# DeltaNet into a noisy top-2 router on one core: own tiles for the first expert's early rows, two tiles of inverses, and a remade plan

## The chip, the cores and the metric

The kernel runs on one core of a Trainium2 chip. The time is device microseconds from the start of the program to its end on that core, a median over runs. One more execution is recorded by the hardware profiler; its own time stands beside the span that its trace covers. All data are fp32.

## The reference

The first half is a DeltaNet recurrence for 4 batches of 8 heads, 768 tokens and head width 48. Its output, laid out as 3072 tokens of 384 numbers, goes to a router with 8 experts, of which each token takes two.

```python
# attention: one state of D x D for each batch and head
k_n = k / (norm(k) + 1e-6)
for t in range(S):
    y[t] = q[t] @ state                     # read before the update
    state += beta[t] * outer(k_n[t], v[t] - k_n[t] @ state)
# router and experts
x = y, as (3072, 384)
noisy = x @ w_gate + log1p(exp(x @ w_noise)) * noise
top2 = the two largest of the 8; weights = softmax over these two
out[token] += weight * (relu(x[token] @ w1[e]) @ w2[e])     # w1: 384 x 1024, w2: 1024 x 384
```

## The kernel before

**Attention.** A chunk holds 64 tokens, there are 12 chunks, and a unit is one chunk of two batches (all their heads), so there are 24 units; four units make a step, `s`, of which there are six. For each step the kernel forms products of the keys (`products`, L558 transposes and L576 matmuls on TensorE, copies at L565, L609 and L615 on ScalarE), and inverts 32 x 32 triangular blocks on VectorE (`begin_inversion`, `invert`, `end_inversion`): one transpose into the tile `t` (L626), a norm (L644 to L665, of which L654 needs `root` from ScalarE, L648 and L649), 30 columns of two operations each (L704, L708), a scaling (L720), and two transposes out (L730 into `tb`, L738 into `tt`). `join` (L761 to L799) puts two such blocks together; `within` gives the masked products of queries and keys (L824); `recur` runs the recurrence (L845 to L928: `solve` is L890, `gather_state` is L912, the state is added at L924), two units at a time; `answer` gives y and the router's logits (L949 to L991; L964 is the matmul of the logits).

**Routing.** `route(g)` turns the logits of one or two steps into experts, weights and row numbers, on VectorE with short matmuls (L1081 to L1087). `spread` (L383, GpSimd) scatters each unit's rows twice, once for each expert, into `rows_x` in device memory: 48 scatters of 128 rows, 1552 bytes each. `cut(s, rows)` makes sure that expert 0 has `rows` rows by then, so that they may be used early.

**Early rows.** `early(s)` takes the first 128-row tiles of expert 0 as soon as the rows of the steps up to `s` are there: load (L1246), transpose (L1274), `hidden = relu(w1 rows)` (L1300, L1310), back through `w2` (L1323), weighting (L1337) and a scatter into the output (L424). In this kernel it works in tiles of the keys and queries that are no longer needed, four tiles at a time and then one:

```python
EARLY = {3: (0, 4), 4: (4, 5)}
xr = old_k[0:4]
xe = [*old_kT[0:2], old_q[0]]
hT = old_k
```

**Order.** Nothing is issued in the order of the source. Each piece is a job with an engine, an estimated cost, what it reads and writes, and a due time; `Jobs.order` simulates the engines with these estimates and writes the order of each engine's queue once, when the program is built. Its constants are `FIRST`, `PACE`, `BEHIND` (due times of inverses and of routing), `SIGNAL` (time from one engine to another), `PATIENCE` and `SOON`. Jobs with `late` set, as those of the early rows, go behind all others that could start. On the chip each engine takes its queue in that order, and a job that waits holds up all behind it; GpSimd's and SyncE's queues are planned in the same way.

**Experts.** After attention, `rest` does the remaining rows of expert 0 and experts 1 to 7 follow, each as a seven-product scheme of block matrices (L1548).

Of the kernel before, what the change touches and what calls it, by code (L numbers as in the profile page):

```python
# [21 lines left out]
Q = 32  # L22
TILES = 6
MORE = 64
EARLY = {3: (0, 4), 4: (4, 5)}
ROWS = TILES * 128 + MORE
ROW = 384 + 4
# [4 lines left out]
FIRST, PACE, BEHIND = 13.0, 36.0, 100.0  # L32
# [60 lines left out]
class Jobs:  # L93
# [8 lines left out]
    SIGNAL = 0.15  # L102
# [5 lines left out]
    def add(self, engine, cost, emit, reads=(), writes=(), opens=None, uses=None, closes=None,  # L108
            lands=0.0, moves=0.0, due=None, late=None, apart=0.0):
        job = SimpleNamespace(  # L110
            engine=engine, cost=cost, emit=emit, opens=opens, closes=closes, lands=lands,
# [105 lines left out]
    PATIENCE = 0.05  # L217
    SOON = 3.0
# [14 lines left out]
def kernel(  # L233
# [148 lines left out]
    def spread(rows, slot, cleared):  # L382
        d = nc.gpsimd.indirect_dma_start(  # L383
            out=rows_x,
            out_offset=bass.IndirectOffsetOnAxis(ap=slot, axis=0),
            in_=rows,
            in_offset=None,
        ).ins
        tc.declare_no_dep(d, group="spread", reason="no two tokens have the same row")
        tc.add_to_no_dep_group("spread", d)  # L390
        for i in cleared:
            tc.add_manual_dep(d, i.name, SYNC, reason="rows cleared before they are written")
        written.append(d)
        return d
# [35 lines left out]
    def deltanet(ictx):  # L430
# [34 lines left out]
        NK, NT_, NW = 3 * US, 3 * US, US + NU  # L465

        NQ, N_U, N_ST = 3 * NU, 2 * NU, 2
# [19 lines left out]
        two_gds = ring([128, UH, Q], "gd", 2)  # L487
        most_steps = max(x for _, x in INVERSIONS)
        inversion_of = {s + x: g for g, (s, n) in enumerate(INVERSIONS) for x in range(n)}
        t_inv = sb([128, most_steps, Q, Q], "t")  # L490
# [94 lines left out]
        def products(n):  # L585
# [15 lines left out]
            gd = two_gds(s).rearrange("p (u j z) i -> p u z j i", u=US, z=2)[:, i]  # L601
            for x, lo in enumerate(range(0, 128, Q)):
# [9 lines left out]
                    writes=[("gd", s % 2, i, lo)], uses=p,  # L612
# [6 lines left out]
        def begin_inversion(s):  # L619
# [3 lines left out]
            gd = two_gds(s)  # L623
# [5 lines left out]
                reads=[("gd", s % 2, i, lo) for i in range(US) for lo in range(0, 128, Q)],  # L629
                writes=["t"], due=FIRST + first_s * PACE + 2 * x,  # L630
            )

        def invert(g):

            first_s, steps = INVERSIONS[g]
            t, v_ = t_inv[:, 0:steps], nc.vector
            diagonal = t.rearrange("p s i j -> p s (i j)")[:, :, 0 : Q * Q : Q + 1]
            ss, root, norm, d, minus_d = (x[:, 0:steps] for x in small.values())
# [28 lines left out]
            jobs.add(DVE, 0.4, squares, reads=["t"], writes=["ss", "root"], due=soon)  # L667
            jobs.add(ACT, 0.5, by_log, writes=["root"], due=soon + 1)

            for x in range(steps):  # L670
# [6 lines left out]
                    reads=["ss"], writes=["t"], due=soon + 3,  # L677
# [3 lines left out]
                DVE, 2.0, lengths, reads=["root", "ss", *every_beta], writes=["norm", "d"],  # L681
                due=soon + 3,
            )
            for x in range(steps):
                jobs.add(
                    DVE, 0.2,
                    lambda x=x: v_.transpose(out=norms(first_s + x), in_=norm[:, x]),
                    reads=["norm"], writes=[("norms", (first_s + x) % 3)],
                )
# [5 lines left out]
                reads=["d"], writes=["t"],  # L695
# [16 lines left out]
            for j in range(1, Q - 1):  # L712
                jobs.add(
                    DVE, 0.36 + 0.0019 * steps * j * (Q - 1 - j), lambda j=j: column(j),
                    writes=["t", *(("column", first_s + x, j) for x in range(steps))],
                )
            jobs.add(DVE, 0.2, lambda: v_.memset(diagonal, 1.0), writes=["t"])
# [5 lines left out]
                reads=["d"], writes=["t"],  # L723
            )

        def end_inversion(s):
            x = s - INVERSIONS[inversion_of[s]][0]
# [6 lines left out]
                reads=["t"], writes=["tb"],  # L734
# [6 lines left out]
                reads=["t"], writes=["tt"],  # L741
            )

        def join(units):
# [21 lines left out]
            for n, m in zip([*units, None], [None, *units]):  # L766
# [34 lines left out]
                jobs.add(PE, 0.65, products_of, reads=reads, opens=p)  # L801
# [134 lines left out]
        def answer(n, bank_y):  # L936
# [64 lines left out]
            x: sb([128, most_steps, Q], x) for x in ("ss", "root", "norm", "d", "minus_d")  # L1001
# [13 lines left out]
        def route(g):  # L1015
# [151 lines left out]
            for x in range(units):  # L1167
                of, i = first_s + x // US, x % US
                for to in slot:
# [4 lines left out]
                            [y for name in clears for y in cleared[name]],  # L1174
# [35 lines left out]
        def flat(t):  # L1210
            return t.rearrange("p h d -> p (h d)")

        def key_of(name, i, size):
            return halves(name, i % size) if name in ("k", "q") else [(name, i % size)]

        def early(s):
# [4 lines left out]
            lo, hi = EARLY[s]  # L1221
            n, rows = hi - lo, (hi - lo) * 128
            first_unit = (NS - 1) * US
            old_k = [(flat(kps(first_unit + US + i)), halves("k", (first_unit + US + i) % NK))
                     for i in range(NK - US)]
            old_kT = [(flat(kTs(first_unit + US + i)), [("kT", (first_unit + US + i) % NT_)])
                      for i in range(NT_ - US)]
            old_q = [(flat(qps(i)), halves("q", i % NQ)) for i in range(NQ)]
            if lo == 0:
                xr = old_k[0:4]  # L1230
                xe = [*old_kT[0:2], old_q[0]]
                hT = old_k
                xr = [(x[:, 0:ROW], key) for x, key in xr]
                hT = [(x[:, 0:rows], key) for x, key in hT]
            else:
                (x, key), (y, key_y), *z = old_kT[2:6]
                xr = [(x[:, 0:ROW], key)]
                xe = [(y[:, do * 128 : (do + 1) * 128], key_y) for do in range(KT)]
                hT = [
                    (z[fo // 4][0][:, fo % 4 * 128 : (fo % 4 + 1) * 128], z[fo // 4][1])  # L1240
                    for fo in range(FT)
                ]

            def load_rows(i):
                r0 = (lo + i) * 128
                d = nc.sync.dma_start(out=xr[i][0], in_=rows_x[r0 : r0 + 128]).ins  # L1246
                for w in written:
                    tc.add_manual_dep(d, w.name, SYNC, reason="rows of the tokens so far")

# [3 lines left out]
            ]  # L1253
            for i in range(n):
                at = lo + i
                jobs.add(
                    SP, 0.7, lambda i=i: load_rows(i), reads=of_steps,
                    writes=[*xr[i][1], ("xr", at)], lands=2.0, moves=0.7, late=lo,
                )

                def of_rows(i=i, at=at):
                    x = xr[i][0]
# [4 lines left out]
                    DVE, 0.5, of_rows, reads=[("xr", at), *xr[i][1]], writes=[("gate", at)],  # L1267
                    late=lo,
                )
                p = Bank(2, (0, 1))  # L1270

                def turned_rows(i=i, p=p):
                    for do in range(KT):
                        nc.tensor.transpose(  # L1274
                            p.tile[:, 0, do * 128 : (do + 1) * 128],
                            xr[i][0][:, do * 128 : (do + 1) * 128], ident,
# [3 lines left out]
                    PE, 0.5, turned_rows, reads=[("xr", at), *xr[i][1]], opens=p, late=lo,  # L1280
                    writes=[k for x in xe for k in x[1]],
                )

                def copied(i=i, p=p):
                    for do in range(KT):
                        nc.scalar.copy(
                            xe[do][0][:, i * 128 : (i + 1) * 128],
                            p.tile[:, 0, do * 128 : (do + 1) * 128],
                        )

                jobs.add(
                    ACT, 0.9, copied,
                    writes=[("xe", at), *(k for x in xe for k in x[1])], closes=p, late=lo,
                )
            for fo in range(FT):
                p = Bank(2, (0, 1))
                for do in range(KT):
                    jobs.add(
                        PE, 0.0017 * rows,
                        lambda fo=fo, do=do, p=p: nc.tensor.matmul(  # L1300
                            p.tile[:, 0, 0:rows], w1e[:, do, fo * 128 : (fo + 1) * 128],
                            xe[do][0][:, 0:rows], start=(do == 0), stop=(do == KT - 1),
                        ),
                        reads=[("xe", lo + i) for i in range(n)] + xe[do][1], late=lo + 0.1,
                        writes=hT[fo][1] if do == 0 else [],
                        **({"uses": p} if do else {"opens": p}),
                    )
                jobs.add(
                    ACT, 0.08 + rows * 0.0011,
                    lambda fo=fo, p=p: nc.scalar.activation(  # L1310
                        hT[fo][0], p.tile[:, 0, 0:rows], ACTF.Relu
                    ),
                    writes=[("hT", lo, fo), *hT[fo][1]], closes=p, late=lo + 0.1,
                )
            for i in range(n):
                at = lo + i
                p = Bank(2, (0, 1))
                got, got_key = old_q[1 + at % 3]
                for f0 in range(0, FT, 2):

                    def back(i=i, p=p, f0=f0):
                        for fo in (f0, f0 + 1):
                            nc.tensor.matmul(  # L1323
                                p.tile[:, 0, 0:DM], hT[fo][0][:, i * 128 : (i + 1) * 128],
# [4 lines left out]
                        PE, 1.3, back, late=lo + 0.2, writes=[] if f0 else got_key,  # L1329
                        reads=[  # L1330
                            x for fo in (f0, f0 + 1) for x in (("hT", lo, fo), *hT[fo][1])
                        ],
# [5 lines left out]
                        got[:, 0:DM], p.tile[:, 0, 0:DM], early_gate[:, at : at + 1]  # L1338
                    ),
                    reads=[("gate", at)], writes=got_key, closes=p, late=lo + 0.2,  # L1340
# [50 lines left out]
        for s in range(NS):  # L1391
# [33 lines left out]
            if s in EARLY:  # L1425
                cut(s, EARLY[s][1] * 128)
# [475 lines left out]
```

## Time and profile before

| what | us |
|---|---|
| median of 3 runs | 885.67 |
| lowest and highest run | 878.36, 887.37 |
| the profiled execution's own time | 881.57 |
| its span | 879.8 |
| TensorE, VectorE, ScalarE, GpSimd busy | 753.7, 564.0, 332.4, 357.0 |
| last matmul of logits (L964) ends | 361.4 |
| early rows on TensorE | 369.0 to 426.3 |
| rest of expert 0 | 427.1 to 447.2 |
| experts 1 to 7 | 447.2 to the end |

Times inside the execution are counted from the start of its span. Engines are PE (TensorE), PEld (its weight loads), DVE (VectorE), ACT (ScalarE), POOL (GpSimd) and SP (SyncE). In the row of slices each digit stands for a fortieth of the span, 22 us. A wait is put down to the engine whose signal came last; "issue" and "remote" are stretches in which the trace shows nothing that the engine waited for, or nothing that it can name.

### The profile page before, as it was taken

How to read it: one execution, taken by the hardware profiler on the slowest of the kernel's cores; microseconds unless marked ns; L12 is line 12 of the kernel's file. 1: busy time of each engine (PE TensorE's matmuls, PEld its weight loads, DVE VectorE, ACT ScalarE, POOL GpSimd, SP SyncE). 2: the span in 40 equal slices, each digit the busy share in tenths (PEclk: the TensorE clock that was granted, in tenths of full speed). 3: DMA queues.
4: the chain of work that ended last, by engine and by line, in shares of the span. 5: the costliest groups of instructions: out<-in, count | busy, mean ns of one | idle time of the engine just before them, and what ended most of it. 6: DMA issues, size and time to landing. Idle time of an engine off the chain costs nothing.

```text
span 879.8 us, 22711 instructions
## 1 busy us (share of the span) xinstructions
PE 753.7 (86%) x9462; PEld 584.6 (66%) x9462; DVE 564.0 (64%) x1297; ACT 332.4 (38%) x791; POOL 357.0 (41%) x372
## 2 busy tenths in 40 slices
PE   3678578765579768799999999999999999999995
PEld 2467467665368657546757858859769678688594
DVE  5889786878559563301479658577587586585651
ACT  3675665735355234220334153152151341431510
POOL 1020202010540341421257487477577675773611
PEclk8578777655859756599999999999999999999998
DMA  2465986833421211371173242433423331401201
GB/s 48 76 122 124 296 179 139 227 83 85 156 80 36 71 65 39 114 261 59 41 256 105 96 145 72 138 104 120 137 80 132 120 104 37 143 3 53 60 19 40
DMA packets 119855, 93.80 MB, mean 107 GB/s; under 512 B 85414, under 2 KB 110023, under 8 KB 119744
## 3 DMA queue, kind: packets, MB, share of 16 engines
q1 hardware_dynamic: 108016, 64.54, 26.6%
q0 software_dynamic: 9552, 27.33, 9.2%
q8 instruction: 76, 1.25, 0.6%
q10 hardware_dynamic: 2176, 0.39, 0.3%
q14 instruction: 35, 0.29, 0.1%
HBM read 58.82 MB, written 34.81 MB: 106 GB/s over the span
## 4 chain that ended last, share of the span: by engine, by line
PE 61%; DVE 13%; issue 7%; ACT 5%; SPq 5%; another core or an unknown queue 4%; POOL 2%; DMA 2%; POOLq 0%; DVEq 0%; ACTq 0%
PE inner L1548 24%; PE outer L1548 14%; DVE part L704 3%; DVE t L708 3%; PE pair L1300 3%; PE pair L1323 3%; PE inner L1653 2%; PE inner L1580 2%; SPq L526 2%; SPq L377 2%; PE pair L890 1%; PE pair L949 1%; PE single L558 1%; PE pair L576 1%
## 5 line engine op out<-in xcount | busy, mean ns | idle before, releaser
L1607 DVE TENSOR_TENSOR hT<-hT,inner 128x416 f32<-128x416 f32 x182 | 105.5, 586 | 61.5 <-PE inner L1548 52.0
L1613 ACT ACTIVATE hT<-inner 128x416 f32<-128x416 f32 x112 | 57.9, 517 | 171.3 <-PE inner L1548 169.1
L424 POOL DMA_INDIRECT out_dram<-sums,index x49 | 50.8, 1037 | 113.7 <-DVE sums L1448 105.3
L673 POOL TENSOR_SCALAR_AFFINE_SELECT t<-t 128x1024 f32<-128x1024 f32 x6 | 7.6, 1266 | 180.9 <-DVE ss L644 180.9
L1548 PE MATMUL inner<-s_x,w1e 128*128 128x416 f32 x196 | 78.7, 512 | 0.0
L1448 DVE SCALAR_TENSOR_TENSOR sums<-outer,gate,sums 128x192 f32<-128x192 f32 x112 | 45.2, 414 | 50.2 <-PE outer L1548 50.1
L708 DVE TENSOR_TENSOR t<-t,part 128x30 f32<-128x30 f32 (+9 forms) x180 | 61.1, 339 | 6.2
L1602 ACT ACTIVATE hT<-hT 128x416 f32<-128x416 f32 x112 | 59.9, 547 | 12.2 <-DVE hT L1607 6.7
L704 DVE TENSOR_TENSOR part<-t 128x30 f32<-128x30 f32 (+9 forms) x180 | 60.2, 334 | 5.1
L1548 PE MATMUL outer<-t_w,hT 128*128 128x192 f32 x336 | 59.7, 328 | 0.0
L383 POOL DMA_INDIRECT rows_x<-y,slot x48 | 46.8, 975 | 28.8 <-issue 11.3
L415 POOL DMA_INDIRECT sums<-out_dram,index x49 | 52.5, 1072 | 13.9 <-issue 13.0
L1548 PE MATMUL inner<-xe,w1e 128*128 128x416 f32 x140 | 58.1, 513 | 0.0
L1548 PEld LDWEIGHTS inner<-s_x,w1e 128*128 128x128 f32 x196 | 37.2, 190 | 31.2 <-issue 29.8
L1548 PE MATMUL inner<-s_x,s_w 128*128 128x416 f32 x140 | 56.9, 512 | 0.0
L1548 PEld LDWEIGHTS outer<-t_w,hT 128*128 128x128 f32 x336 | 54.7, 190 | 0.4
L1585 ACT COPY xe<-inner 128x384 f32<-128x384 f32 (+1 forms) x49 | 20.1, 462 | 85.4 <-PE inner L1580 85.4
L1548 PE MATMUL outer<-w2e,hT 128*128 128x192 f32 x280 | 50.1, 326 | 0.0
L1548 PEld LDWEIGHTS outer<-w2e,hT 128*128 128x128 f32 x280 | 46.5, 190 | 2.2 <-issue 2.2
L1514 POOL TENSOR_TENSOR w1e<-w1e 128x256 f32<-128x256 f32 x54 | 46.3, 867 | 2.0
L558 PE MATMUL single<-ident,kp 128*128 128x128 f32 x96 | 22.7, 380 | 23.7 <-DMA kp<-in_k_dram 14.7
L1548 PEld LDWEIGHTS inner<-s_x,s_w 128*128 128x128 f32 x140 | 26.6, 190 | 22.3 <-issue 22.3
(220 smaller groups left out, 1650.8 us busy)
## 6 DMA issues: line engine op xcount, KB each, us to landing
w1e<-in_moe_w_dram SPq DMA_DIRECT2D x8, 1536.0 KB
w2e<-in_moe_w_dram SPq DMA_DIRECT2D x8, 1536.0 KB
xr<-rows_x SPq DMA_DIRECT2D x7, 1164.0 KB
rows_x<-empty SPq DMA_DIRECT2D x8, 776.0 KB
v<-in_v_dram SPq DMA_DIRECT2D x48, 96.0 KB
qp<-in_q_dram SPq DMA_DIRECT2D x48, 96.0 KB
out_dram<-empty SPq DMA_DIRECT2D x4, 1152.0 KB
kp<-in_k_dram SPq DMA_DIRECT2D x88, 48.0 KB
```

The lines of the kernel that those rows point to most:

```text
L383: d = nc.gpsimd.indirect_dma_start(out=rows_x, out_offset=bass.IndirectOffsetOnAxis(ap=slot, axis=0), in_=rows, in_offset=None,).ins
L415: nc.gpsimd.indirect_dma_start(out=got, out_offset=None, in_=out, in_offset=bass.IndirectOffsetOnAxis(ap=index, axis=0), bounds_check=N - ...
L424: nc.gpsimd.indirect_dma_start(out=out, out_offset=bass.IndirectOffsetOnAxis(ap=index, axis=0), in_=got, in_offset=None, bounds_check=N - ...
L558: nc.tensor.transpose(p_t[:, j], src(n)[:, 2 * j : 2 * j + 2], ident)
L704: v_.tensor_tensor(out=part, in0=t[:, :, j + 1 :, j, None].to_broadcast(shape), in1=t[:, :, None, j, 0:j].to_broadcast(shape), op=ALU.mult,)
L708: v_.tensor_tensor(out=t[:, :, j + 1 :, 0:j], in0=t[:, :, j + 1 :, 0:j], in1=part, op=ALU.add)
L1448: nc.vector.scalar_tensor_tensor(out=got, in0=p, scalar=gate, in1=got, op0=ALU.mult, op1=ALU.add)
L1514: engine.tensor_tensor(out=block(to), in0=block(x), in1=block(y), op=ALU.add if sign == "+" else ALU.subtract,)
L1548: nc.tensor.matmul(p, lhsT, rhs, start=opens and i == 0, stop=i == len(products) - 1, skip_group_check=True,)
L1602: nc.scalar.activation(h, h, ACTF.Relu)
L1607: nc.vector.tensor_tensor(out=h, in0=h, in1=p, op=ALU.add if sign > 0 else ALU.subtract)
L1613: nc.scalar.mul(h, p, float(sign))
```

## The change

- The early rows get tiles of their own, `early_x` (four, also used for the results), `early_xe` and `early_hT`, and go in batches of two, two and one 128-row tiles. All three pairs of PSUM banks are open to them. A load waits for the scatters of the steps up to `s`, no longer for all scatters that were issued by then.
- The room comes from smaller rings: queries and values (with their transposes and masked products) from 6 to 4, transposed keys from 12 to 11, and one tile `gd` in place of two.
- The tile of inverses `t` and its small companions are doubled (`t_invs`, `small`), so that one step's inverse may be begun before the one before is finished and taken out.
- The constants of the plan are changed, matmuls are given 1.3 times their cost in it, and the order of all queues is remade.

```diff
-EARLY = {3: (0, 4), 4: (4, 5)}
+EARLY_BANK = 2, (0, 1, 2)
+EARLY = {3: [(0, 2), (2, 4)], 4: [(4, 5)]}
+EARLY_TILES = 5
...
-FIRST, PACE, BEHIND = 13.0, 36.0, 100.0
+FIRST, PACE, BEHIND = 15.0, 44.0, 110.0
...
-    SIGNAL = 0.15
+    SIGNAL = 0.4
+    SLOW = 1.3
...
-            engine=engine, cost=cost, emit=emit, opens=opens, closes=closes, lands=lands,
+            engine=engine, cost=cost * (self.SLOW if engine == self.PE else 1.0), emit=emit, opens=opens, closes=closes, lands=lands,
...
-    PATIENCE = 0.05
-    SOON = 3.0
+    PATIENCE = 0.02
+    SOON = 8.0
...
-        NK, NT_, NW = 3 * US, 3 * US, US + NU
+        NK, NT_, NW = 3 * US, 3 * US - 1, US + NU
...
-        NQ, N_U, N_ST = 3 * NU, 2 * NU, 2
+        NQ, N_U, N_ST = 2 * NU, 2 * NU, 2
...
-        two_gds = ring([128, UH, Q], "gd", 2)
+        gd_all = sb([128, UH, Q], "gd")
...
-        t_inv = sb([128, most_steps, Q, Q], "t")
+        t_invs = ring([128, most_steps, Q, Q], "t", 2)
...
-            x: sb([128, most_steps, Q], x) for x in ("ss", "root", "norm", "d", "minus_d")
+            x: ring([128, most_steps, Q], x, 2) for x in ("ss", "root", "norm", "d", "minus_d")
...
+        early_x = [sb([128, ROW], f"early_x{i}") for i in range(4)]
+        early_xe = sb([128, KT, 256], "early_xe")
+        early_hT = sb([128, FT, 256], "early_hT")
...
+            def load_rows(at):
+                d = nc.sync.dma_start(
+                    out=early_x[at % 4], in_=rows_x[at * 128 : (at + 1) * 128]
+                ).ins
+                for of, w in written:
+                    if of <= s:
+                        tc.add_manual_dep(d, w.name, SYNC, reason="rows of the tokens so far")
...
+            for fo in range(FT):
+                p = early_bank()
+
+                def inner_of(fo=fo, p=p):
                     for do in range(KT):
+                        nc.tensor.matmul(
+                            flat(p)[:, 0:rows], w1e[:, do, fo * 128 : (fo + 1) * 128],
+                            early_xe[:, do, 0:rows], start=(do == 0), stop=(do == KT - 1),
                         )
...
-        for s in EARLY:
-            early(s)
+        for s, batches in EARLY.items():
+            for lo, hi in batches:
+                early(s, lo, hi)
```

## The prediction

> **What bounds the kernel now.** I read the row of slices first, then the waits of VectorE in attention, then the timeline at its longest waits.
>
> ```profile
> PE   3678578765579768799999999999999999999995
> DVE  5889786878559563301479658577587586585651
> PEclk8578777655859756599999999999999999999998
> ```
>
> Each digit is 22 us. From slice 17 on TensorE is full: early rows, the rest of expert 0, seven experts. Before that no engine is full; TensorE and VectorE stand near 7 tenths with gaps, in queues whose order is fixed. The 452.4 us behind 427.1 are the same instructions in both kernels, so the change is decided before 427 us. What VectorE's gaps waited for, in the stretches 20 to 200, 200 to 290 and 290 to 372 us (in total, times, longest):
>
> ```profile
> DVE norm L654 <- ACT root L649: 10.1, 4, 4.7
> ...
> DVE t L626 <- ACT gd L609: 16.0, 1, 16.0
> DVE norm L654 <- ACT root L649: 4.8, 2, 4.3
> DVE st L924 <- ACT y L975: 1.9, 1, 1.9
> ...
> DVE st L924 <- remote: 15.5, 1, 15.5
> ```
>
> So 14.9 us in six waits of the norm for ScalarE's root, and two single waits of 16.0 and 15.5 us. What stood around the second, on GpSimd and on TensorE:
>
> ```profile
> 299.48 0.99 POOL L383 DMA_INDIRECT rows_x<-y,slot  x1 [4.61 <-DVE r_count L1109]
> 300.78 0.96 POOL L383 DMA_INDIRECT rows_x<-y,slot  x1 [0.30 <-issue]
> 302.04 0.96 POOL L383 DMA_INDIRECT rows_x<-y,slot  x1 [0.30 <-issue]
> ...
> 303.79 0.48 PE L912 MATMUL pair<-u,kp 64*64 64x48 f32 x5 [0.28 <-issue]
> 305.25 0.45 PE L912 MATMUL pair<-u,kp 64*64 64x48 f32 x4 [0.99 <-issue]
> 306.70 0.46 PE L912 MATMUL pair<-u,kp 64*64 64x48 f32 x4 [1.00 <-issue]
> ```
>
> While GpSimd scatters rows one behind the other (11 from 299.5 to 313.1 us; before that 13 from 229.0 to 247.0), TensorE gets four or five matmuls and then waits up to 1 us for nothing the trace names, so that 32 matmuls which take 0.85 to 1.1 us elsewhere take 6. I take it that the scatters starve the other engines; whatever the mechanism, a burst costs what stands behind it. The third view is the end of attention:
>
> ```profile
> 355.00:361.00 6.00, 6.00 (x101) 5.38 (x94) 0.00 (x0) 2.56 (x6) 2.50 (x3) 0.50 0.31 108
> 361.00:367.00 6.00, 0.53 (x3) 0.45 (x4) 4.19 (x25) 1.06 (x5) 4.22 (x5) 0.50 0.38 143
> 367.00:372.00 5.00, 4.95 (x22) 4.09 (x22) 2.94 (x23) 1.73 (x9) 1.18 (x2) 0.50 0.10 40
> ```
>
> (stretch, length, then busy time of PE, PEld, DVE, ACT, POOL, and the granted clock). TensorE stands still from 361.4 to 366.8 us, while VectorE finds the experts of the last tokens.
>
> **Early rows.** "Among the last chunks" is not what the changed program's queue has. Two transposes (L1274 before) stand ahead of the last logits; the third and 36 matmul instructions (six of the eight hidden blocks of the first batch) stand between these and the last routing matmuls; everything else comes after them. So the only gap they can fill is that of 5.4 us. The work itself is the same: before, the instructions take 21.6 (48 of 512 columns), 20.6 (64 of 384), 5.6 (48 of 128) and 5.2 us (16 of 384), and two batches of 256 columns have 96 instructions at half the 0.45 us, again 21.6. After the logits: 36 x 0.225 = 8.1 us cover the 5.4, so the gap goes. [...] Net **-3 us**.
>
> [...] The row nearest in this trace is the fifth tile, 48 instructions of 128 columns in 5.59 us, 116 ns each; a quarter of the 512-column instruction's 451 ns would be 113, so 3 ns are lost, 0.1 us for the 48. [...]
>
> The loads of early rows no longer wait for attention's tiles: before, they were issued at 352 us; now they can go when the scatters of step 3 have landed, which in the old trace is near 335 us. That has 25 us in hand before the transposes need it; without that cover the transposes would hold up the last logits behind them. The fifth tile's load now waits for the scatter of the first result, which stands on GpSimd behind all eight last row scatters: about 25 us after the logits, with SyncE's load of expert 1's weights queued behind it. Before, these were issued at 382.9 us, 21.5 after the logits. They are needed some 65 us after, so the 4 us cost nothing.
>
> **Two tiles of inverses.** VectorE's work is the same. Counting the queue of each program with the rows' means (0.335 us a column operation, 1.2 a scaling, 1.95 a transpose, 0.55 a state or value operation, 0.68 a mask), VectorE has done 38, 76, 112, 151, 188 and 239 us of work when it starts L730 for the six steps before, and 48, 77, 114, 158, 195 and 239 in the changed order. What moves are the waits.
> - The root: between its source (L645) and L654 the new order puts, for steps 1 to 4, two column pairs and a mask (2.0 us), six column operations (2.2), a transpose out (2.0), and four column operations with a state (1.9). Against waits of 2.2, 4.7, 2.6 and 4.3 this hides 8.1; step 5 gets a further 3.3 for its 0.5. Bounds 0 (ScalarE is late by as much again) and 14. **-9 us**.
> - The wait of 16.0: keys of step 5 were transposed and copied behind the first burst (ScalarE's copies at 234.9 and 248.2 us). Now their matmuls stand ahead of the second half of step 3, and GpSimd puts that burst into step 3, with the four values' multiplies (L854) in between. When it starts, VectorE has about 10 us of work (a transpose out, a scaling, columns of step 4) before it needs what TensorE makes in it, of a burst of 18 us. Of 17.9 us (with the 1.9 behind it) 8 to 10 remain. Bounds 0 and 18. **-8 us**.
> - The wait of 15.5: routing of steps 2 and 3 ends at the same place, 11 scatters still follow each other before the next multiply, and VectorE still has little but a scaling and a transpose before the next state. **0**.
>
> **What it costs.** Four query and value tiles for six: SyncE's load of the next value stands behind the `solve` of a unit four earlier, and the loads of keys behind it. TensorE already waits 12.3 us for keys and 4.9 for queries up to 372 us. I bound the new wait by 0 and by 15 (nearly as much again) and take **+4**, near the low end, since four units are a whole step of 40 to 50 us. Two transposes more ahead of the last logits cover ground that is needed anyway: 0.
>
> Sum: -3 -9 -8 +4 = **-16 us**. Against the profiled execution's 881.6 this is 865.6; the median of the runs lies 4.1 above that one, and leaning to it I say **867**.
>
> **Rivals.**
> - *The waits only change their names* (no change, about 879): six states and values wait for TensorE instead of for the root, and the burst costs step 3 what it cost step 4. For it: a burst slows TensorE wherever it falls. Then only the -3 is left. Range 874 to 884.
> - *The first step comes late* (slower, 894): ahead of the first norms (L687), which let GpSimd and then the recurrence start, the new order puts a second norm (2.0), a scaling (1.2), 20 short column operations (5.6), two masks (1.4) and a third transpose in (1.9): 45.9 us of VectorE's work become 58.8, and the first `solve`, at 66.8 us, starts 12.9 later. It decides if TensorE cannot make it up: its busy time from 70 to 360 us is 211 of 290, so 79 are idle, but much of that is in chains. With nothing made up and the -3: 881.6 + 12.9 - 3 = 891.5, and half the rings' upper bound brings it near 894. Against it: from the second step on the states stand in VectorE's queue no later than before (the seventh pair at 183 and 185 us of work, before 201 and 203).
> - *Both bursts are covered* (845): the first fully (9 more) and most of the second (12 more), if VectorE's longer lead in columns holds. Against it: same neighbours in the queue at the second.
>
> **How the numbers follow.** The forecast's case 0.46, its own range 855 to 876; no change 0.18; late start 0.24; both covered 0.12. From 846 to 896 holds eight in ten: below it most of half of the last case, above it the worst of the late start. One per cent, 8.8 us, is about what a measurement of this kernel tells from no change. Faster by over 1%: nearly all of the first case (0.42), all of the last (0.12), in sum 0.54. Within 1%: 0.04 of the first, 0.15 of no change, 0.02 of the late start, 0.21. Slower: 0.22 of the late start and 0.03 of no change, 0.25.
>
> **What would show it.** Right: L654's waits for L649 at 6 us or less in sum; no wait of L626 over 3 us; the stretch from the last L964 to the rest of expert 0 at 62 to 63 us for 65.7; the 15 us wait of a state for "remote" still there. Wrong: that stretch unchanged or longer, or the last L964 at or after 361 us, with TensorE or VectorE waiting for loads of values or for the first norms; the first `solve` later than 67 us by 13, and not made up by the fourth step.

## The result and the profile after

The changed kernel takes **853.05 us** (median of 4 runs, 849.53 to 861.25) against 885.39 for the kernel before on the same chip (4 runs, 878.36 to 887.37): 0.9647 of the time, 95% interval 0.9563 to 0.973. It is faster by 32.3 us, where the prediction's sum was 16 and its number 867. The profiled execution took 852.83 us, its span is 851.1; all times below are counted from the start of the span. Some executions of a kernel take over 1.5% longer than its fastest one, and all medians and ranges below leave these out (with them the kernel with one inverse tile would stand at 879, the number that later expectations name).

The row of slices first; a slice is now 21.3 us.

```profile
PE   3656888877878488999999999999999999999995
...
PEclk8565576785697769999999999999999999999998
```

TensorE's row is full from slice 16 on where it was full from 17 (the first slice is 0), and there is one deep hole left in it (the 4 at slice 13). The granted clock stays at 9 from slice 15 to the last but one; before it was 5, 6 and 5 in slices 14 to 16. What VectorE waited for in the changed kernel, in the stretches 20 to 200, 200 to 290 and 290 to 345 us:

```profile
DVE st L931 <- PE pair L919: 13.2, 6, 5.6
...
DVE norm L660 <- ACT root L655: 0.6, 1, 0.6
DVE t L629 <- ACT gd L612: 0.4, 1, 0.4
...
DVE v L881 <- PE pair L579: 13.0, 2, 12.5
...
DVE missing L1194 <- remote: 11.1, 1, 11.1
```

The waits for the root (14.9 us before) are gone, and so is the 16.0 us wait of `t` for `gd`. In their places stand six waits of a state for TensorE (13.2 us), a value's wait of 12.5 us and a wait of 11.1 us for nothing that the trace can name. These last two waits lie in the two bursts of row scatters (15 from 193.0 to 216.1 us and 11 from 285.1 to 298.9). The second burst, from the timelines of GpSimd, ScalarE, TensorE and VectorE:

```profile
285.09 1.02 POOL L386 DMA_INDIRECT rows_x<-y,slot  x1 [4.69 <-DVE r_count L1116]
...
284.80 0.65 PE L897 MATMUL pair<-v,w 64*64 64x48 f32 x32
285.38 0.38 PE L1204 MATMUL single<-before,ones 128*128 128x1 f32 x2
285.62 0.75 PE L561 MATMUL single<-ident,qp 128*128 128x128 f32 x4
298.26 0.99 PE L956 MATMUL pair<-u,qk 64*64 64x48 f32 x26 [11.88 <-issue]
...
297.73 0.48 ACT L908 COPY u<-pair 128x384 f32<-128x384 f32 x1 [12.20 <-remote]
...
287.98 0.22 DVE L714 TENSOR_TENSOR t<-t,part 128x58 f32<-128x58 f32 x1
299.35 0.15 DVE L1194 TENSOR_SCALAR missing<-single 1x1 f32<-1x1 f32 x1 [11.15 <-remote]
```

Read the starts. The matmuls of L897 and L1204 were over at 285.45 and 285.76. The copy (L908) that needs the first ran at 297.73, and the operation (L1194) that needs the second at 299.35. So ScalarE and VectorE stood for 11 to 12 us with what they needed long made. TensorE stood as long, but it isn't shown that it could have gone on: its next matmuls (L956) need the `u` that L908 makes, and they start at 298.26, just after that copy ended at 298.21. The profile's word "issue" doesn't tell the two cases apart.

The third place is the end of attention. The timeline of TensorE behind the last logits (L971, over at 340.5), then the whole stretch up to the rest of expert 0 (length, busy PE, PEld, DVE, ACT, POOL, granted clock, DMA share, GB/s):

```profile
340.33 0.52 PE L1265 MATMUL pair<-ident,early_x 128*128 128x128 f32 x3
340.69 6.64 PE L1284 MATMUL pair<-early_xe,w1e 128*128 128x256 f32 x30
348.22 1.56 PE L1284 MATMUL pair<-early_xe,w1e 128*128 128x256 f32 x6 [0.90 <-ACT early_hT L1295]
```

```profile
340.50:397.20 56.70, 54.61 (x243) 40.65 (x243) 8.94 (x41) 10.40 (x32) 17.46 (x19) 1.00 0.44 155
```

36 early matmuls, up to the routing's matmul (L1088) at 349.62, now fill the place where TensorE stood for 5.4 us, the longest pause is 0.90, and the clock is 1.00 all through. Landmarks in the two profiled executions (us):

| | before | after |
|---|---|---|
| first norms (L687, L693 after) | 56.6 | 70.3 |
| first `solve` (L890, L897) | 66.8 | 72.3 |
| transpose into `tb` (L730, L737), six steps | 49.3, 91.3, 134.2, 184.0, 229.0, 317.3 | 58.9, 92.3, 137.1, 189.4, 244.5, 301.4 |
| last matmul of logits ends | 361.4 | 340.5 |
| first matmul of the rest of expert 0 (L1483, L1467) | 426.1 | 397.2 |

Up to the fifth step the changed kernel is late (9.6, 1.0, 2.9, 5.4, 15.5 us); then it gains 31.5 us within one step. Of the 28.9 us at the rest of expert 0, 20.9 are there at the last logits and 8.0 arise behind them. What follows takes 454 us in both.

### The profile page after: what moved, and what is told of

It reads as the page before. It is cut to its first block, busy times and chain, and to the rows that moved or that the text cites. A ratio compares the mean times of both kernels' runs of the same rounds, so it can differ in the third digit from the quotient of the medians.

```text
span 851.1 us, 22812 instructions
## 1 busy us (share of the span) xinstructions
PE 744.6 (87%) x9510; PEld 586.4 (69%) x9510; DVE 567.7 (67%) x1295; ACT 331.7 (39%) x789; POOL 359.5 (42%) x372
## 4 chain that ended last, share of the span: by engine, by line
PE 45%; issue 5%; POOL 2%; ACT 0%; POOLq 0%; ACTq 0%
PE inner L1532 24%; PE outer L1532 15%; PE inner L1637 2%; PE inner L1564 2%; POOL out_dram L427 1%; PE inner L1675 1%; POOL sums L418 1%; PE outer L1685 1%; POOL t_w L1505 0%; PE outer L1690 0%; PE outer L1675 0%; PE outer L1664 0%; ACT xe_r L1668 0%; ACT hT L1679 0%; POOLq L418 0%
## 5 line engine op out<-in xcount | busy, mean ns | idle before, releaser
L710 DVE TENSOR_TENSOR part<-t 128x30 f32<-128x30 f32 (+9 forms) x180 | 66.8, 371 | 4.5
L714 DVE TENSOR_TENSOR t<-t,part 128x30 f32<-128x30 f32 (+9 forms) x180 | 64.1, 356 | 6.2
L1586 ACT ACTIVATE hT<-hT 128x416 f32<-128x416 f32 x112 | 59.9, 547 | 12.2 <-DVE hT L1591 7.0
L679 POOL TENSOR_SCALAR_AFFINE_SELECT t<-t 128x1024 f32<-128x1024 f32 x6 | 7.6, 1267 | 134.2 <-DVE ss L650 134.2
L861 POOL TENSOR_TENSOR v<-v,norms 128x384 f32<-128x384 f32 x24 | 22.2, 941 | 69.6 <-DVE norms L693 29.9
```

The source lines that it names most:

```text
L710: v_.tensor_tensor(out=part, in0=t[:, :, j + 1 :, j, None].to_broadcast(shape), in1=t[:, :, None, j, 0:j].to_broadcast(shape), op=ALU.mult,)
L714: v_.tensor_tensor(out=t[:, :, j + 1 :, 0:j], in0=t[:, :, j + 1 :, 0:j], in1=part, op=ALU.add)
L861: lambda: [nc.gpsimd.tensor_tensor(out=v_n, in0=v_n, in1=norms(s)[:, i * H : (i + 1) * H, None].to_broadcast([128, H, D]), op=ALU.mult,)],
L1586: nc.scalar.activation(h, h, ACTF.Relu)
```

## The experiments

The table gathers the times. All kernels were timed against the kernel before on their own chip; the ratio is to it. "Logits" and "rest" are the last two landmarks above, in the profiled execution. The kernels without row scatters don't compute the result, so only their times up to the last logits are to be compared. For two kernels only the times are used. A profiled execution lies up to 7 us from its kernel's median (before, new constants: 6.8 below; changed, one inverse tile: 7.2 above), so a few us between the landmarks of two kernels are not safe.

| kernel | median us | ratio, 95% interval | logits | rest |
|---|---|---|---|---|
| before | 885.39 | 1 | 361.4 | 426.1 |
| changed | 853.05 | 0.9647 (0.9563 to 0.973) | 340.5 | 397.2 |
| before, new constants | 868.22 | 0.9856 (0.9781 to 0.9932) | 340.9 | 405.6 |
| changed, old constants | 893.54 | 1.0131 (1.0055 to 1.0206) | 380.1 | 438.9 |
| changed, one inverse tile | 874.85 | 0.9907 (0.9862 to 0.9952) | 365.5 | 422.6 |
| changed, old early rows | 856.55 | 0.9716 (0.9645 to 0.9786) | 338.3 | 398.6 |
| two inverse tiles, order of one | 871.38 | 0.9875 (0.9767 to 0.9984) | | |
| one inverse tile, two `gd` | 865.23 | 0.9792 (0.9699 to 0.9884) | 348.4 | 409.1 |
| changed, no row scatters | 829.14 | 0.9366 (0.9254 to 0.9477) | 316.5 | 372.1 |
| before, no row scatters | 849.75 | 0.9598 (0.9504 to 0.9693) | 322.4 | 388.6 |
| changed, old costs | 888.06 | 1.0061 (1.0012 to 1.011) | 382.2 | 436.2 |
| changed, old due times | 873.61 | 0.9936 (0.9875 to 0.9997) | | |
| changed, scatters apart | 856.62 | 0.9723 (0.9603 to 0.9842) | 344.2 | 401.3 |
| two inverse tiles, two `gd` | 880.13 | 0.9983 (0.9932 to 1.0034) | 361.0 | 425.3 |

The first theory (the tiles theory) is the prediction's: two tiles of inverses take VectorE's waits away, own early tiles fill the gap. The rival (the plan theory): the constants, which remake the order, bring the gain.

### Constants alone, and tiles alone

The first puts the new constants into the kernel before:

```diff
-FIRST, PACE, BEHIND = 13.0, 36.0, 100.0
+FIRST, PACE, BEHIND = 15.0, 44.0, 110.0
...
-    SIGNAL = 0.15
+    SIGNAL = 0.4
+    SLOW = 1.3
...
-            engine=engine, cost=cost, emit=emit, opens=opens, closes=closes, lands=lands,
+            engine=engine, cost=cost * (self.SLOW if engine == self.PE else 1.0), emit=emit, opens=opens, closes=closes, lands=lands,
...
-    PATIENCE = 0.05
-    SOON = 3.0
+    PATIENCE = 0.02
+    SOON = 8.0
...
-                jobs.add(PE, 0.65, products_of, reads=reads, opens=p)
+                jobs.add(PE, 0.75, products_of, reads=reads, opens=p)
```

> The kernel before with the new constants of the plan alone (FIRST, PACE, BEHIND, SIGNAL, SLOW, PATIENCE, SOON, products at 0.75): one tile of inverses, old early rows, old rings. If the two tiles of inverses bring the gain (tiles theory), this stays at 880 to 890 us, with the root waits of L654 still 10 to 15 us in sum. If the remade plan brings it (plan theory), this falls to 860 to 868 us, and the waits of 16.0 and 15.5 us get shorter while the root waits stay. If neither does alone, because the order is only good where tiles and constants go together (joint theory), it may even be slower than 890.

Measured 868.22 us, 15.6 below the kernel before on that chip (883.83), so by the medians half of the change's 32 comes with no tile changed at all. By the ratio it is 1.4% of the change's 3.5%, with an interval from 0.7 to 2.2%. The profiled execution was the fastest of its four (861.45); in it the last logits end at 340.9, where the changed kernel has 340.5, and the stretch behind them is as long as before (64.7 us). VectorE's waits from 20 to 345 us:

```profile
DVE qk L825 <- remote: 9.8, 1, 9.8
DVE st L925 <- remote: 7.6, 1, 7.6
...
DVE norm L655 <- ACT root L650: 4.2, 5, 1.6
```

The two waits of 16.0 and 15.5 have become 9.8 and 7.6; the root's waits are 7.3 in sum (3.1 more at L649), half of the 14.9, with one tile of inverses; the plan theory had them stay.

The second is the mirror: the changed kernel with those lines set back.

> The changed kernel with the old constants of the plan: two tiles of inverses, own early tiles and smaller rings stay. Tiles theory: 853 to 860 us, root waits of L660 under 3 us in sum. Plan theory: 872 to 885 us, with one or two waits of VectorE of 15 us or more back around the bursts of scatters. Joint theory: anything above 875.

Measured 893.54 us, 1.3% slower than the kernel before. All tiles of the change are there, and with this order they do not help. Its waits of VectorE, 20 to 380 us:

```profile
DVE st L931 <- PE pair L919: 27.0, 11, 9.0
DVE v L881 <- remote: 13.8, 1, 13.8
...
```

States wait for TensorE eleven times. The tiles theory fails in both runs (880 to 890 and 853 to 860 were its numbers). The plan theory's number for the first is met at its edge; the second is above its 872 to 885, so it is not the constants alone either: tiles, rings and constants make an order together.

### One tile of inverses, and a second one that the order does not use

```diff
-        t_invs = ring([128, most_steps, Q, Q], "t", 2)
+        t_invs = ring([128, most_steps, Q, Q], "t", 1)
...
-                (x, g % 2) for x in ("t", "d", "norm", "ss", "root")
+                (x, 0) for x in ("t", "d", "norm", "ss", "root")
...
-            x: ring([128, most_steps, Q], x, 2) for x in ("ss", "root", "norm", "d", "minus_d")
+            x: ring([128, most_steps, Q], x, 1) for x in ("ss", "root", "norm", "d", "minus_d")
```

> The changed kernel with one tile of inverses and one set of its small companions instead of two; constants, rings and early rows stay. Tiles theory: 865 to 875 us: 9 to 14 us of root waits come back and the inverse of a step cannot begin before the last one is taken out. Plan theory: 853 to 858 us, with root waits back in the trace but other waits shorter by as much. The first norms should come earlier than at 70.3 us (near 58) in both.

Measured 874.85 us over seven runs (871.51 to 882.53): within the changed kernel the second tile is worth 22 us. The number is the tiles theory's (865 to 875), its cause is not. The first norms do come early again (55.7 us). But only 5.8 us of root waits came back:

```profile
...
DVE missing L1194 <- remote: 11.6, 1, 11.6
...
DVE norm L660 <- ACT root L655: 5.8, 4, 4.5
```

So the tile's worth is not its root waits. The next kernel has two tiles in SBUF, and is planned as if there were one:

```diff
-                reads=[("t", inversion_of[s] % 2)], writes=["tb"],
+                reads=[("t", 0)], writes=["tb"],
...
-                (x, g % 2) for x in ("t", "d", "norm", "ss", "root")
+                (x, 0) for x in ("t", "d", "norm", "ss", "root")
```

> Two tiles of inverses in SBUF, but planned as if there were one, so that every engine's queue is exactly that of the run with one tile. If the second tile helps by taking waits away in a given order, this is several us faster than the 879 of one tile, and near the 853 of the changed kernel if that is all of it. If it helps only by the other order that it lets the plan write, this stays at 876 to 882, with the last logits again at 365 us.

Measured 871.38 us over three runs (869.42 to 882.04), ratio 0.9875 (0.9767 to 0.9984), where one tile had 0.9907 (0.9862 to 0.9952). The intervals lie on each other. A second tile in an unchanged order does nothing that can be told from none; what it brings beyond that, it brings by the order that the plan may then write.

### What a second `gd` does

The changed kernel also made `gd` single. With one `t` as well, keys of the next step cannot be copied until `t` is taken out. This kernel has one `t`, by the first edit above, and two `gd`:

```diff
-        gd_all = sb([128, UH, Q], "gd")
+        two_gds = ring([128, UH, Q], "gd", 2)
...
-                    writes=[("gd", i, lo)], uses=p,
+                    writes=[("gd", s % 2, i, lo)], uses=p,
```

> One tile of inverses as in the run of 879 us, and two tiles gd instead of one (the room is the same as in the changed kernel: gd and the second inverse tile are both 4 KB); new constants, smaller rings of queries and values, own early rows. If what hurts with one inverse tile is that gd is single as well (the copies of the next step's keys must wait until t has been taken out and gd transposed), the last logits end at 340 to 345 us and the time is 853 to 860. If the smaller rings or the own early rows hurt, it stays at 875 to 882 with the last logits near 365. If a second inverse tile is needed for itself, 865 to 880.

Measured 865.23 us, logits at 348.4: 9.6 us of the 22 come back. That is the lower edge of the third case (865 to 880), with logits between those of the first and the second. The other one has two of both, with the ring of transposed keys cut to 10 and early rows to 3 tiles for the room (the lines of `gd` are as above):

```diff
-        NK, NT_, NW = 3 * US, 3 * US - 1, US + NU
+        NK, NT_, NW = 3 * US, 3 * US - 2, US + NU
...
-        early_x = [sb([128, ROW], f"early_x{i}") for i in range(4)]
+        early_x = [sb([128, ROW], f"early_x{i}") for i in range(3)]
```

> The changed kernel with two tiles gd as well as two tiles of inverses; room for it from transposed keys (10 for 11) and early rows (3 tiles for 4). If the single gd still costs something in the changed kernel (keys of the next step copied late), the last logits end before 338 us and the time is 843 to 850. If two inverse tiles make the second gd worthless, 851 to 857. If the smaller ring of keys hurts more, over 860.

Measured 880.13 us, 27 slower than the changed kernel, with logits at 361.0. Whether the smaller rings do it or the order that came out isn't told apart by this run. With the same constants, the arrangements of the same work in this table lie between 853 and 880 us, and the room given does not sort them.

### Old early rows

The changed kernel with `early` as it was before, in old keys' and queries' room, four tiles and then one:

```diff
-EARLY = {3: [(0, 2), (2, 4)], 4: [(4, 5)]}
+EARLY = {3: (0, 4), 4: (4, 5)}
...
+                xr = old_k[0:4]
+                xe = [*old_kT[0:2], old_q[0]]
+                hT = old_k
```

> The changed kernel with the old early rows: four tiles and then one, in the room of old keys and queries, two pairs of banks; two tiles of inverses, constants and smaller rings stay. If the own room is worth what the two traces show behind the last logits (65.7 to 57.7 us), this is 7 to 9 us slower than the changed kernel: 859 to 863 us, with TensorE standing still for some 5 us behind the last logits and a stretch of 64 to 66 us from the last L971 to the rest of expert 0. If the prediction's -3 is right and the rest of the 8 us is the clock of the last steps, 855 to 857 us and a stretch of 60 to 62. The end of the logits itself should stay within 2 us of 340.5.

Measured 856.55 us, 3.5 over the changed kernel; the intervals of the two overlap, so the size is not safe by the times. In the traces the stretch behind the logits is 3.6 us longer, though the logits themselves end 2.2 us earlier (338.3 for 340.5). From the last logits to the rest of expert 0:

```profile
338.30:398.60 60.30, 56.73 (x199) 32.47 (x198) 9.00 (x41) 10.16 (x33) 17.65 (x19) 0.97 0.44 146
```

60.3 us for 56.7 after and 64.7 before, so the second theory's 60 to 62. TensorE idles 3.6 us of it (6.3 before, 2.1 after), and is busy for 56.7 (58.4 before, 54.6 after): of the 3.6 us to the changed kernel, 1.5 are idle time and 2.1 longer busy time, at a clock of 0.97 where it was 0.90 before and is 1.00 after. Here the clock came in at 1.00 and fell: behind a pause of 1.90 us and a few short matmuls (343.73 to 345.0) it was 0.64 from 346 to 350 us, with TensorE busy throughout.

### Without the row scatters

Each scatter becomes a memset of one column; queues stay as they are. The rows that the experts read stay cleared, so what comes behind the last logits is not computed.

```diff
-        d = nc.gpsimd.indirect_dma_start(
-            out=rows_x,
-            out_offset=bass.IndirectOffsetOnAxis(ap=slot, axis=0),
-            in_=rows,
-            in_offset=None,
-        ).ins
+        d = nc.gpsimd.memset(nothing, 0.0).ins
```

> The changed kernel with each of the 48 row scatters replaced by a memset of one column on GpSimd; all queues stay in their order. The rows that the experts read stay cleared, so only the time up to the last logits is to be compared. Starving theory (a burst of scatters slows the other engines): TensorE's 15.6 us of waits for issue at L956 and the 12.5 and 11.1 us waits of VectorE go to under 4 us each, and the last logits end at 315 to 328 us for 340.5. Coincidence theory (those waits come from the order of queues and what TensorE still had to do): the last logits end within 5 us of 340.5.

> The kernel before with the same replacement of its 48 row scatters, all queues in their order; only the time up to the last logits is to be compared. Starving theory: the waits of 16.0 us (t for gd) and 15.5 us (state for remote) go to under 4 us each, and the last logits end at 330 to 345 us for 361.4. If the changed kernel's gain is that its plan covers the bursts better, the two kernels without scatters end their logits within 5 us of each other; if the gain is elsewhere, about 20 us stay between them. Coincidence theory: within 5 us of 361.4.

The last logits end at 316.5 us in the changed kernel (24.0 earlier) and at 322.4 in the kernel before (39.0 earlier). The first is in the starving theory's range; the second is 7.6 us below its 330 to 345, so the scatters cost more there than it had. Coincidence is out. The other execution of the changed kernel without scatters, which was not profiled, took 8.2 us less than the profiled one. The same stretches of time with and without scatters, where a burst was (columns as above). The changed kernel:

```profile
205.00:218.00 13.00, 6.10 (x59) 4.04 (x58) 0.61 (x2) 1.10 (x3) 8.79 (x10) 0.50 0.69 245
284.00:299.00 15.00, 3.12 (x100) 2.67 (x100) 3.75 (x17) 1.30 (x4) 10.71 (x11) 0.67 0.46 152
```

The same without its scatters:

```profile
205.00:218.00 13.00, 8.73 (x286) 7.80 (x289) 11.05 (x30) 7.73 (x20) 0.00 (x0) 0.77 0.44 128
284.00:299.00 15.00, 13.84 (x550) 12.30 (x545) 6.12 (x25) 14.00 (x37) 3.64 (x11) 0.73 0.02 4
```

In the same 15 us TensorE runs 550 matmuls without the burst and 100 with it, ScalarE 37 operations and 4. The kernel without scatters is 11.7 us further on in its work there, so it is the rate that may be compared. How late the scatters make each landmark (time with scatters less time without, us):

| | `tb` steps 1 to 4 | `tb` step 5 | `t` for step 6 (L626) | `tb` step 6 | logits |
|---|---|---|---|---|---|
| before | -1.2 to 1.0 | 2.2 | 16.0 | 31.3 | 39.0 |
| changed | under 0.1 | 11.7 | 11.7 | 23.0 | 24.0 |

The steps in these rows are the waits in the profile: 16.0 and then 15.3 before, where VectorE waited 16.0 and 15.5; 11.7 and 11.3 after, where it waited 12.5 and 11.1. In these two kernels a wait inside a burst was lost in full, and nothing of it was made up later. Before, a further 7.7 us went with the last step; after, 1.0.

Between the two kernels 5.9 us remain at the logits when no rows are scattered, near the 5 that the expectation gave for a plan that covers the bursts better, and far from 20. The kernel before then still has nearly all its root waits:

```profile
DVE norm L649 <- ACT root L644: 13.8, 6, 4.2
```

So **15.0 of the 20.9 us at the logits are what the remade order saves in the bursts and behind them**, and some 6 come from root waits with all else that it moved. That is by one trace of each kernel. If all the 8.2 us between the two executions named above lay ahead of the logits, some 7 us would be saved in the bursts and some 14 elsewhere.

### Which constants

The changed kernel with the costs alone set back:

```diff
-    SIGNAL = 0.4
-    SLOW = 1.3
+    SIGNAL = 0.15
+    SLOW = 1.0
...
-                jobs.add(PE, 0.75, products_of, reads=reads, opens=p)
+                jobs.add(PE, 0.65, products_of, reads=reads, opens=p)
```

> The changed kernel with only the constants of cost set back: SIGNAL 0.15, SLOW 1.0, products 0.65; due times, PATIENCE and SOON stay new. With all constants old the time was 893.5. If the cost model is what the new plan lives on (it makes the plan expect TensorE to be late, so that it puts more of VectorE's work ahead of what TensorE makes), this is 875 to 893. If the due times are, 853 to 862.

And with the due times and the choice among ready jobs alone set back:

```diff
-FIRST, PACE, BEHIND = 15.0, 44.0, 110.0
+FIRST, PACE, BEHIND = 13.0, 36.0, 100.0
...
-    PATIENCE = 0.02
-    SOON = 8.0
+    PATIENCE = 0.05
+    SOON = 3.0
```

> The changed kernel with only FIRST, PACE, BEHIND, PATIENCE and SOON set back; SIGNAL, SLOW and the products' cost stay new. If the cost model carries the gain, 853 to 862; if the due times do (44 for 36 us a step, which lie nearer to the 45 to 50 that a step takes), 875 to 893. If the two halves share the 40 us, both runs lie near 870.

Measured 888.06 and 873.61 us; both set back gave 893.54 and neither 853.05. Setting back either half alone loses 35 or 21 us, so they are not two gains that add up. The loss with old costs is larger, but neither theory fits both runs, and the shared one (both near 870) doesn't either.

### Scatters further apart

```diff
-                        due=FIRST + (s + paced) * PACE + BEHIND + 5.0, apart=4.5 / steps * paced,
+                        due=FIRST + (s + paced) * PACE + BEHIND + 5.0, apart=(9.0 if g == 0 else 4.5) / steps * paced,
```

> The changed kernel with the row scatters of the first two steps planned 4.5 us apart for 2.25, so that its first eight do not follow each other but have values' multiplies between them; the second burst still has 10 in a row. If a burst costs by its density, the wait of 12.5 us at L881 goes to under 6 and the last logits end 4 to 8 us earlier: 845 to 850 us. If each scatter costs the others the same wherever it stands, no change: 851 to 856. If the remade order is worse elsewhere, over 860.

Measured 856.62 us, no change that can be told. The edit didn't reach its aim: by the profile the starts of 13 scatters still lie within 19.6 us (191.4 to 211.0), as those of the first 13 in the changed kernel do, and VectorE still waits 11.3 us at L881. Whether a thinned burst costs less stays open. No kernel tried here beats the changed one.

## Why the prediction was right, and where its sum was not

Direction and range held; the size was half of what came. Of the signs that it named, two came true: L654's waits are 0.6 us (6 or less) and that of L626 0.4 (3 or less). The stretch behind the logits went past its mark, with 57.7 by its measure for 62 to 63. The fourth came true in part: a wait for "remote" is still in the second burst, with 11.1 us for 15, but at the `cut` of the rows and not at a state. (One figure of its first part is off: behind 427.1 us stand 452.7 of the span, not 452.4.) By its own steps, at the rest of expert 0, where the profiled executions differ by 28.9:

| step | forecast | measured | from |
|---|---|---|---|
| early rows, stretch behind the logits | -3 | -8.0 | 64.7 to 56.7 us |
| root waits and rings | -9 and +4 | -5.9 together | the two kernels without scatters |
| first burst | -8 | -4.3 | 16.0 to 11.7 |
| second burst | 0 | -4.0 | 15.3 to 11.3 |
| last step, its eight or nine scatters | not in the sum | -6.7 | 7.7 to 1.0 |

The rows of the bursts and of the roots come from one trace of each kernel, with the caution of the section on the scatters.

**Early rows.** The gap was read rightly: it is gone, and TensorE's idle time in the stretch fell by 4.2 us (6.3 to 2.1). The -3 is the gap's 5.4 us less some 0.4 for one more wait and 1.7 for work at a granted clock of 0.50; no run shows the 1.7. In its place TensorE's busy time fell by 3.8 us (58.4 to 54.6), at a clock of 1.00 for 0.90. In the kernel before the clock came into the stretch at 0.50 (it fell between 350 and 351 us), stayed there through the pause of 5.4 us and until 374 us, 7 us of TensorE's work behind it; now it comes in at 1.00 and no pause is over 0.90 us. The forecast took the 0.50 for given in any order of the queues. What decides the clock is not shown: with old early rows it fell behind a pause of 1.90 us, and from 354.35 to 361.4 us before, TensorE was busy without a pause at 0.50, for 7.0 us. Halving the batch cost TensorE no busy time: 30 instructions of 256 columns in 6.64 us are 221 ns each, no more than half of the old 451.

With old early rows the stretch is 60.3, so 3.6 of the 8.0 go with the own room, near the 3 of the forecast. The other 4.4 are there without it; that kernel too comes in at a clock of 1.00, and its pauses are shorter (3.6 us in all for 6.3). That the higher clock brings the 4.4 is likely and not shown.

**Root waits and rings.** The waits went further than forecast (14.3 of 14.9 us, 9 were forecast). But a wait that goes is not a gain of its size: without scatters, 13.8 us of root waits in one kernel and 0.6 in the other are worth 5.9 us together with the rest. The +4 for smaller rings has no wait behind it: TensorE's waits for keys fell from 12.3 to 7.7 us and for queries from 4.9 to 3.2. That the sum of -5 came near is luck: one part was too large and the other had no ground.

**Bursts.** That a burst costs what stands behind it was right, and so was the place: without its scatters 16.0 us come back at the first burst in the kernel before and 11.7 in the changed one, at the second 15.3 and 11.3. The first burst was put at -8 and brought -4.3. VectorE had the work for it that was counted (busy for 9.6 us between 193.0 and 205.6, for 10). But the burst took 23 us for 18: it has 15 scatters for 13, and four multiplies stand between them. VectorE stood 12.5 us of it. The second was put at 0, as its neighbours were the same; it brought 4.0, and five column pairs of the last inverse that VectorE worked off in it (285.2 to 288.2 us) are 3.0 of these. A third term was missing, that of the scatters and the low clock behind the second burst. From the sixth `tb` to the last logits the kernel before took 44.1 us at a granted 0.62, with nine scatters, and the changed one 39.1 at 0.85, with eight; without scatters these steps take 36.4 and 38.1. The runs do not part clock and scatters there.

**The cause.** The largest error is in whose work it was. The prediction read its waits from the changed queue, in which tiles and constants act together, wrote -17 under "Two tiles of inverses", and gave the constants no term. With the old constants the tiles make the kernel slower (893.54), and the constants alone bring 15.6 us without them. What the second tile does is to let another order be written: with the smaller rings, a single `gd` and one tile the median is 874.85, with two tiles 853.05, and with the larger rings, one tile and the new constants 868.22. So with these constants the second tile more than buys back what the room for early rows costs. No run has two tiles and the larger rings, and why one order is better than another is known here only as far as the bursts and waits above show it.

**The rivals.** "The first step comes late" happened, at a lower price: the first norms came 13.7 us later (12.9 were counted, though the five items listed for it add up to 12.1), the first `solve` only 5.5. It was not made up by the fourth step, which the text had named as proof against the forecast; it was 15.5 us late at the fifth, and ahead at the sixth. The test failed because the fourth step lies before the bursts. "The waits only change their names" is true of what one sees in the list (13.2 us of states waiting for TensorE), not of the time. "Both bursts are covered" named a right cause for a gain above the forecast: with what stands behind them they are cheaper by 15.0 us, but 24.0 are still lost.

## What to carry to other kernels

Where a program writes the order of its queues from cost estimates, test the estimates by themselves before crediting a buffer: here new constants on old tiles brought some two fifths to half of the gain, new tiles on old constants a loss, and a second tile in an unchanged order nothing. Take a suspected burst out and compare landmarks: it shows what a wait is worth, which the list of waits alone does not (16.0 us in a burst were lost in full, some 13 us of root waits were worth about 6). A wait named "issue" may still be one for an operand: compare the end of its producer with the start of its consumer. And look at the busy time where a pause goes: at the end of attention 1.5 us of idle time and 2.1 of busy time went with the old early rows, with the granted clock at 0.97 with them and 1.00 without.

## What was unexpected of the hardware

In the second burst, 11 scatters in 13.8 us, ScalarE and VectorE stood for 12.2 and 11.1 us with their operands ready, and TensorE, whose next operand ScalarE was to make, for 11.9. The first burst still let TensorE through at four to six matmuls per 1.45 us, where it stopped in the midst of a group of matmuls. Without the scatters the same 15 us had 550 matmuls.

It is not only in bursts that TensorE stops so. In the changed kernel without scatters it also stopped in the midst of a group of 32, behind its second matmul, while VectorE worked on. The first two rows are TensorE's; the last is of the DMA queues from 85.66 to 90.57 us (packets, MB, share of the DMA engines):

```profile
85.21 0.45 PE L847 MATMUL pair<-st,qT 64*64 64x48 f32 x2
90.57 0.99 PE L847 MATMUL pair<-st,qT 64*64 64x48 f32 x28 [4.91 <-issue]
...
q1 hardware_dynamic: 750, 1.04, 98.8%
```

In these 4.9 us no scatter ran, and other transfers kept the DMA engines busy. So a stop of this kind needs no scatter; whether it is the same in the bursts is not shown.

The profile has queues of the kind "instruction". From 285 to 300 us they moved no packet in the changed kernel. Without the scatters they moved four (the DMA queues of that kernel in these 15 us):

```profile
q8 instruction: 4, 0.07, 1.6%
```

Whether the packets have to do with the stop is not shown; ScalarE, TensorE and VectorE went on at 297.73, 298.26 and 299.35, ahead of the next such packet that the trace has (300.0 to 300.5 us).
